# Decoding in the attention stage ordered for later transfers, a hand-over filled with input products, and output chains that go on as activations come

## The chip, the core and the metric

The kernel runs on one core of one Trainium2 chip. Five engines work side by side, each through a queue of its own: PE (TensorE, matmuls; its weight loads are PEld), DVE (VectorE), ACT (ScalarE), POOL (GpSimd) and SP (SyncE, which here only issues transfers). The metric is the device time of one execution in microseconds.

## What is computed

```python
def rmsnorm(x, g): return x / sqrt(mean(x * x, -1) + 1e-06) * g
q_n, k_n = rmsnorm(q, g_q), rmsnorm(k, g_k)            # (4, 12, 448, 64)
attn = softmax(q_n @ k_n.T / 8) @ v
x = attn.transpose(0, 2, 1, 3).reshape(1792, 768)
x = relu(x @ w_in) ** 2 @ w_out                        # layer 1: 768 -> 2048 -> 768
out = silu(x @ w_gate) * (x @ w_val) @ w_out2          # layer 2: 768 -> 1536 -> 768
```

Everything is float32. The products keep float32 accuracy: each operand is split into a rounded high part and a low rest, and each product is three matmuls (`mm3`: high by high, high by low, low by high).

## The kernel before

**Stages.** In the attention stage (0 to about 416 us) 24 pairs of heads are worked through: scores `sc`, a softmax whose exponentials go into `ring`, transposes `pt` that are copied into `turned_p`, the values product `o`, and `ox`, the normed result, which is stored and split into `x`. PE has time to spare there, and it is filled with layer 1's first six blocks of 128 inner columns for batches 0 to 2 (`fillers`, `ffn1a`: `h_a` and `ya`). Batch 3's blocks 0 to 2 end that filling (`lead`: `h_lead` twice, then `lead`). After this hand-over `products` finishes batch 3: for block `f` an input product `h`, a squared ReLU (`squares`: ReLU on ACT, L405; square on ACT, L406; ReLU times ReLU on DVE, L407, which frees the bank of `h`; the low rest on DVE, L411), and output products `y` into six banks (`first_out`). Then come 14 passes over what is left of layer 1 and all of layer 2, each over two batches at once with Strassen's seven products (`unit`: `p1` to `p7`, from sums of weights `s`, `a` and sums of tokens `t`, `b`). A pass ends with its output products (`outputs`): twelve chains of `y`, one for each of six column blocks `j` and two batches `h`. A chain adds up the contributions of all units of the pass, in the order of `deep`; the activation of a unit, row and batch is an `s_...` tile whose low part DVE writes last (L1691, layer 2: L1138).

**Word loads and decoding.** The weights arrive as 64-bit words. `word_chunk` loads 128 x 384 of them (`raw_...`, 384 KB, one of two buffers) and decodes them in place in four steps (L1163 or L1165, L1169, L1172, L1179); the last writes a part tile, of which `DEC_TEMPS` may be in use. `combine` adds part tiles (L1143) to the sums that the seven products need, and `keep` stores each part in DRAM, from where the passes read it back. `decode_ahead` does this for the passes' weights from the attention stage on, behind everything else.

**What sets the order.** The code is made of threads that ask for instructions with a cost each; a planner (`simulate`, `dispatch`) with a clock of its own hands them to the engines, lowest rank first, and the order in which it does so is the order of each engine's queue on the chip. An engine takes its queue strictly in this order. A transfer counts in the planner as `max(dma_free, clock + 1100) + bytes / 300 + 900 + later` ns: the fourth element of what `dma` yields is `later`, used once the attention stage has begun to lend PE to the fillers (`lent`). A thread that yields a condition goes on when it holds on the planner's clock. `ranked` is set at the hand-over.

**Names.** `led`, `DEC_LATER` and `AHEAD` do not exist yet. In `outputs` (L1711) the first four or six chains are begun up to the last element of `deep`, those of batch 0 first, then each chain is ended in turn. Eight banks of PSUM serve `p` and `y`; `h_free` lists the free ones.

Of the kernel before, what the change touches and what calls it, by code (L numbers as in the profile page):

```python
# [54 lines left out]
KEEP = {"q": 2, "x": 3, "p": 3, "y": 1, "u": 0}  # L55
DEC_AHEAD = 2
DEC_FROM = 0
DEC_TEMPS = 3
POOL_DMA = 900
POOL_LATER = 2500  # L60
BEHIND = 2
# [22 lines left out]
WC = 384  # L84
# [4 lines left out]
def attention_two_ffn_kernel(  # L89
# [77 lines left out]
    def spawn(gen, rank, is_local=False):  # L167
        t = Thread(gen, rank, is_local)
        local[is_local] += 1
        resume(t, None)  # L170
        return t
# [32 lines left out]
    port, port_last, ranked = [0.0], [], []  # L204
# [61 lines left out]
    def dma(issue, nbytes, later=0):  # L266
        while not ranked and nbytes >= DMA_BULK and dma_free[0] > clock[0] + 1100 + DMA_QUEUE:
            yield dma_free[0] - clock[0] - 1100 - DMA_QUEUE
        yield {"S": 475}, issue, nbytes, later if lent else 0
# [34 lines left out]
    wt, placed, seen = {}, {}, set()  # L304
# [84 lines left out]
    def h_tile(name):  # L389
        yield lambda: h_free  # L390
        where = h_free.pop(0)
        return tile_at(where, [128, S], F32, name), where
# [629 lines left out]
    def lead():  # L1022

        x = x1[B - 1]
        hs = []
        for f in range(2):
            hs.append((yield from h_tile(f"h_lead{f}")))
        parts = [(0, range(KD - 1)), (1, range(KD - 1)), (0, [KD - 1]), (1, [KD - 1]), (2, range(KD))]
        for n, (f, part) in enumerate(parts):
            if n == LEAD_HOLD:  # L1030
                leading.append(0)
            if f == 2:
                yield lambda: acc_last[0] == NH - 1 and t_banks
                where = t_banks.pop(0)
                hs.append((tile_at(where, [128, S], F32, "lead2"), where))
            for kk in part:
                yield lambda: kk in x
                yield from mm3(
                    hs[f][0], *wt["in", f], bass.ts(kk, 128), x[kk][:, 0, :], x[kk][:, 1, :], kk == 0, kk == KD - 1
                )  # L1040
            if part[-1] == KD - 1:
                spawn(squares(*hs[f], f"1_0_{f}"), 9000, FILL if f == 2 else False)
        yield lambda: "1_0_1" in ready
        leading.clear()

# [31 lines left out]
            h_free.append(next(w for w in t_banks if w[0] is ps_f))  # L1077
            t_banks.remove(h_free[-1])

    filled, lent = [], []  # L1080

    def all_stats():
        for b in range(B):
# [73 lines left out]
    def word_chunk(src, c, raw_at, name, parts):  # L1157
        src = src.bitcast(I32).rearrange("p (n two) -> p n two", two=2)
        raw = raw_at[0].tile([128, WC, 2], I32, tag=raw_at[1], name=f"raw_{name}")
        yield from dma(lambda e: e.dma_start(out=raw, in_=src[:, bass.ts(c, WC), :]), 8 * WC * 128)  # L1160
        high, low = raw[:, :, 1], raw[:, :, 0]
        yield {"A": 455, "W": 269}, lambda e: (
            e.activation(out=high.bitcast(F32), in_=high.bitcast(F32), func=ACTF.Copy, scale=2.0 ** -112)  # L1163
            if e is nc.scalar
            else e.tensor_scalar(  # L1165
                out=high.bitcast(F32), in0=high.bitcast(F32), scalar1=2.0 ** -112, scalar2=None, op0=ALU.mult
            )
        )
        yield {"W": 269}, lambda e: e.tensor_scalar(  # L1169
            out=low, in0=low.bitcast(U32), scalar1=2.0 ** -29, scalar2=7.0, op0=ALU.mult, op1=ALU.min  # L1170
        )
        yield {"W": 469}, lambda e: e.scalar_tensor_tensor(  # L1172
            out=low, in0=high, scalar=SIGN_BIT, in1=low, op0=ALU.bitwise_and, op1=ALU.bitwise_or
        )
        yield lambda: ahead_of[0] < DEC_TEMPS
        ahead_of[0] += 1
        at = yield from temp()
        t = tile_at(at, [128, WC], F32, name)
        yield {"W": 469}, lambda e: e.scalar_tensor_tensor(  # L1179
            out=t.bitcast(I32), in0=high, scalar=3, in1=low, op0=ALU.logical_shift_left, op1=ALU.bitwise_or  # L1180
        )
        raws.append(raw_at)
        parts[name] = t, at
# [18 lines left out]
        back(at)  # L1202

    def keep(key, name, t):
        yield from dma(lambda e: e.dma_start(out=pre_d[key][name], in_=t), 4 * WC * 128)
        kept.add((name, key))

    def keep_out(key, name, parts):
# [264 lines left out]
    def products():  # L1473
        k = POST
        xs = x1[LAST]
        behind, ys = [], {}
        for f in range(G1):
            name = f"1_0_{f}"
            if f < 3:
                release(("in", f))  # L1480
            else:
                ps, where = yield from h_tile(f"h_{name}")
                yield from in_product(ps, wt["in", f], xs)
                spawn(squares(ps, where, name), k - 2)
                release(("in", f))
            while len(behind) >= BEHIND:
                yield from behind.pop(0)
            behind.append(first_out(name, f, ys, k))
            k += 1
        for j in range(6):  # L1490
            s_free.append((xp, f"x{j}"))
        for gen in behind:
            yield from gen
        io_free.extend(ea_free)
        yield from all_passes()
        finished.append(0)
# [214 lines left out]
    def outputs(n, sums, drop_w, k):  # L1711
        layer, p, us = passes[n]
        deep = depth(layer, us)
        ahead = 4 if len(deep) > 2 else 6
        ys = {}
        y_order = order_of(n)
        last_use = {j // 3: m for m, (j, h) in enumerate(y_order)}

        def chain(j, h, part):
            ps = ys[j, h][0]  # L1720
            for u, r in part:
                name = f"o{2 * r + j // 3}"
                yield lambda: ((layer, u), name) in operand and (n, u, r, h) in ready
                w, s = operand[(layer, u), name][0], ready[n, u, r, h][0]
                yield from mm3(
                    ps, w[:, 0], w[:, 1], bass.ts(j % 3, 128), s[:, 0], s[:, 1],
                    (u, r) == deep[0], (u, r) == deep[-1],
                )

        for j, h in sorted(y_order[:ahead], key=lambda jh: jh[1]):  # L1730
            ys[j, h] = yield from bank_tile(f"y_{n}_{j}_{h}")
            yield from chain(j, h, deep[:-1])
        for m, (j, h) in enumerate(y_order):
            if m >= ahead:
                ys[j, h] = yield from bank_tile(f"y_{n}_{j}_{h}")
            yield from chain(j, h, deep[-1:] if m < ahead else deep)
            spawn(summed_out(n, j, h, ys[j, h], sums), k)
            if m == last_use[j // 3] and drop_w:
                for u, r in deep:
                    w_free.append(operand.pop(((layer, u), f"o{2 * r + j // 3}"))[1])  # L1740
        for u, r in deep:
            for h in range(2):
                s_free.append(ready.pop((n, u, r, h))[1])
# [118 lines left out]
```

## Time and profile before

| | |
|---|---|
| median of 3 runs | 1242.45 us (1241.45 to 1244.17) |
| profiled execution | 1242.65 us, span 1240.7 us |
| PE busy | 1199.1 us, 97% of the span, 6336 matmuls |
| DVE, ACT, POOL busy | 919.5, 705.0, 289.9 us |
| DMA | 271.69 MB, mean 219 GB/s |
| chain that ended last | PE 69%, DVE 10%, DMA 9%, ACT 7% |

A busy share is an average over stages. The page models the ends of matmuls: one of 448 columns is shown 0.37 us long while the next starts 0.20 us after it, so short pauses of PE do not all show. For an engine's wait the page names the instruction or transfer that came last before it.

### The profile page before, as it was taken

How to read it: one execution, taken by the hardware profiler on the slowest of the kernel's cores; microseconds unless marked ns; L12 is line 12 of the kernel's file. 1: busy time of each engine (PE TensorE's matmuls, PEld its weight loads, DVE VectorE, ACT ScalarE, POOL GpSimd, SP SyncE). 2: the span in 40 equal slices, each digit the busy share in tenths (PEclk: the TensorE clock that was granted, in tenths of full speed). 3: DMA queues.
4: the chain of work that ended last, by engine and by line, in shares of the span. 5: the costliest groups of instructions: out<-in, count | busy, mean ns of one | idle time of the engine just before them, and what ended most of it. 6: DMA issues, size and time to landing. Idle time of an engine off the chain costs nothing.

```text
span 1240.7 us, 20299 instructions
## 1 busy us (share of the span) xinstructions
PE 1199.1 (97%) x6336; PEld 1017.5 (82%) x6336; DVE 919.5 (74%) x1877; ACT 705.0 (57%) x1550; POOL 289.9 (23%) x411
## 2 busy tenths in 40 slices
PE   8989999999999899999999999999999999999998
PEld 6656667676767799999889989998999899989998
DVE  7998987786777697493659798786767577857744
ACT  6999877676767465454654353644453446344310
POOL 4454454433321002313430000110031305030000
PEclk9999999999999999999999999999999999999999
DMA  7576667667747879959897898967695889797714
GB/s 222 167 210 177 189 198 225 183 193 228 220 151 210 258 255 312 212 161 258 193 232 266 271 323 265 307 216 231 207 271 148 225 226 242 196 236 222 266 46 141
DMA packets 169694, 271.69 MB, mean 219 GB/s; under 512 B 25633, under 2 KB 149170, under 8 KB 169586
## 3 DMA queue, kind: packets, MB, share of 16 engines
q1 hardware_dynamic: 155762, 248.37, 63.4%
q0 software_dynamic: 13824, 22.03, 10.9%
q8 instruction: 50, 0.82, 0.3%
q14 instruction: 58, 0.48, 0.1%
HBM read 177.57 MB, written 92.74 MB: 218 GB/s over the span
## 4 chain that ended last, share of the span: by engine, by line
PE 69%; DVE 10%; DMA 9%; ACT 7%; issue 3%; SPq 1%; POOL 0%; DVEq 0%; ACTq 0%; POOLq 0%
PE p L370 32%; PE y L370 26%; ACT ring L808 3%; DMA raw_a<-in_w_in_dram 2%; PE ya L370 2%; PE o L937 2%; PE h_a L370 2%; PE sc L766 2%; DMA raw_o<-in_w_out_dram 2%; DVE sc L794 2%; ACT turned_p L262 1%; PE pt L897 1%; DMA a_d<-a 1%; PE h L370 1%; DMA nat<-in_k_n_dram 1%
## 5 line engine op out<-in xcount | busy, mean ns | idle before, releaser
L370 PE MATMUL y<-s,o_split 128*128 128x448 f32 x1584 | 326.2, 366 | 6.0 <-DVE s L1691 3.2
L370 PEld LDWEIGHTS y<-s,o_split 128*128 128x128 f32 x1584 | 296.8, 188 | 33.2 <-DVE s L1138 4.7
L1599 DVE TENSOR_TENSOR u<-p,u 128x448 f32<-128x448 f32 x204 | 124.2, 618 | 118.5 <-PE p L370 113.7
L370 PE MATMUL p<-t,s_split 128*128 128x448 f32 x918 | 205.4, 368 | 0.0
L370 PEld LDWEIGHTS p<-t,s_split 128*128 128x128 f32 x918 | 172.5, 188 | 16.2
L370 PE MATMUL p<-b,a_split 128*128 128x448 f32 x612 | 137.0, 368 | 0.0
L808 ACT ACTIVATE ring<-sc,m,rms 128x448 f32<-128x448 f32 x168 | 124.1, 743 | 8.8 <-DVE m L795 5.1
L370 PEld LDWEIGHTS p<-b,a_split 128*128 128x128 f32 x612 | 115.0, 188 | 10.5
L1759 ACT COPY yw<-y 128x448 f32<-128x448 f32 x120 | 63.3, 535 | 77.2 <-PE y L370 68.7
L794 DVE TENSOR_REDUCE sc<-sc 128x2 f32<-128x896 f32 (+1 forms) x96 | 93.7, 976 | 6.1 <-PE sc L766 5.2
L262 ACT COPY turned_p<-pt 128x384 f32<-128x384 f32 (+2 forms) x168 | 89.0, 544 | 13.5 <-PE pt L897 13.0
L897 PE MATMUL pt<-ident,ring 128*128 128x128 f32 x432 | 71.3, 276 | 9.3 <-DVE ox L959 4.9
L937 PE MATMUL o<-turned_p,v 128*64 128x448 f32 x384 | 79.8, 546 | 0.6 <-DVE turned_p L264 0.5
L370 PE MATMUL h_a<-x,hi_in 128*128 128x448 f32 x216 | 70.5, 389 | 0.0
L370 PE MATMUL ya<-sa,hi_out 128*128 128x448 f32 x216 | 69.5, 385 | 0.0
L897 PEld LDWEIGHTS pt<-ident,ring 128*128 128x128 f32 x432 | 52.0, 141 | 20.8 <-DVE ox L959 6.8
L370 PE MATMUL p<-t,a_split 128*128 128x448 f32 x306 | 68.8, 369 | 0.0
L370 PE MATMUL p<-b,s_split 128*128 128x448 f32 x306 | 68.3, 367 | 0.0
L1774 POOL DMA_DIRECT2D y2d<-yw x48 | 41.8, 919 | 92.3 <-ACT yw L1759 86.7
L370 PEld LDWEIGHTS p<-t,a_split 128*128 128x128 f32 x306 | 57.5, 188 | 5.7
L370 PEld LDWEIGHTS p<-b,s_split 128*128 128x128 f32 x306 | 57.5, 188 | 5.6
L1138 DVE TENSOR_TENSOR t<-t 128x448 fp32r<-128x448 f32 x87 | 50.6, 618 | 14.8 <-ACT t L262 14.6
(181 smaller groups left out, 2148.7 us busy)
## 6 DMA issues: line engine op xcount, KB each, us to landing
t<-t_d SPq DMA_DIRECT2D x96, 224.0 KB
raw_o<-in_w_out_dram SPq DMA_DIRECT2D x44, 384.0 KB
s_d<-a SPq DMA_DIRECT2D x68, 192.0 KB
s_split<-s_d SPq DMA_DIRECT2D x68, 192.0 KB
b<-x1d SPq DMA_DIRECT2D x51, 224.0 KB
kq<-in_kq_p_dram SPq DMA_DIRECT2D x23, 480.0 KB
y1d<-yw POOLq DMA_DIRECT2D x48, 224.0 KB, 7.7
y2d<-yw POOLq DMA_DIRECT2D x48, 224.0 KB, 7.2
```

Source lines behind the costliest of these rows:

```text
L262: e.copy(out, src)
L370: return {"P": 203}, lambda e: e.matmul(ps, lhsT=w, rhs=x, start=first, stop=last), 0
L766: e.matmul(parts[t][:, :S], lhsT=q[a][d, bass.ts(i % 4, 128)], rhs=k[c][d], start=(p == 0), stop=(p == len(passes) - 1),)
L794: e.tensor_reduce(out=top, in_=sc, axis=AX.X, op=ALU.max, negate=True)
L808: yield {"A": 704}, lambda e: e.activation(out=slot(i), in_=parts[t][:, :S], func=ACTF.Exp, bias=m[:, t:t + 1], scale=rq[:, i:i + 1], accu ...
L897: e.transpose(ps[:, bass.ts(j + (i > 3), 128)], p[:, bass.ts(j, 128)], ident)
L937: e.matmul(o[64 * h:64 * h + 64], lhsT=v[:, 4 * h + j], rhs=turned_p[:, 4 * h + j if j < 3 else 3], start=(j == 0), stop=(j == 3),)
L1138: yield {"W": 469 if c == WC else 535, "G": 956 if c == WC else 1106}, lambda e: e.tensor_tensor(out=t[:, 1], in0=plain, in1=as_f32(t[:, 0 ...
L1599: return {"V": 535}, lambda e: e.tensor_tensor(out=out, in0=ps, in1=b, op=ALU.add)
L1759: yield {"A": 424}, lambda e: e.copy(y, ps)
L1774: yield {"G": POOL_DMA}, lambda e: e.dma_start(out=dst, in_=y, accum_op=ALU.add), 2 * 128 * S * 4, POOL_LATER, True
```

## The change

Three things. **1.** `word_chunk` and `keep` pass `later = DEC_LATER = 1500` ns for their transfers until the hand-over, so that the planner takes them to land 1.5 us later; and four part tiles may be in use instead of three. **2.** `lead` adds the input product of block 3 of batch 3 behind the third lead chain and leaves its bank in `led`; `products` takes it from there when it comes to `f == 3`. **3.** `outputs` no longer begins a set number of chains: up to six chains are open; whenever an open chain's next activation and weights are there on the planner's clock, the oldest such chain goes on; else the next chain is opened if a bank is free.

```diff
-DEC_TEMPS = 3
+DEC_TEMPS = 4
+DEC_LATER = 1500
+AHEAD = 6
...  lead()
                 spawn(squares(*hs[f], f"1_0_{f}"), 9000, FILL if f == 2 else False)
+        ps, where = yield from h_tile("h_1_0_3")
+        yield from in_product(ps, wt["in", 3], x)
+        led.append((ps, where))
         yield lambda: "1_0_1" in ready
...  word_chunk()
-        yield from dma(lambda e: e.dma_start(out=raw, in_=src[:, bass.ts(c, WC), :]), 8 * WC * 128)
+        yield from dma(lambda e: e.dma_start(out=raw, in_=src[:, bass.ts(c, WC), :]), 8 * WC * 128, 0 if ranked else DEC_LATER)
...  keep()
-        yield from dma(lambda e: e.dma_start(out=pre_d[key][name], in_=t), 4 * WC * 128)
+        yield from dma(lambda e: e.dma_start(out=pre_d[key][name], in_=t), 4 * WC * 128, 0 if ranked else DEC_LATER)
...  products()
-                ps, where = yield from h_tile(f"h_{name}")
-                yield from in_product(ps, wt["in", f], xs)
+                if led:
+                    ps, where = led.pop()
+                else:
+                    ps, where = yield from h_tile(f"h_{name}")
+                    yield from in_product(ps, wt["in", f], xs)
...  outputs(): the two loops over y_order and chain() are replaced
+        todo, open_, left = list(order_of(n)), {}, {}
...
+        def can(j, h):
+            u, r = deep[open_[j, h][1]]
+            return ((layer, u), f"o{2 * r + j // 3}") in operand and (n, u, r, h) in ready
+
+        while todo or open_:
+            at = next((jh for jh in open_ if can(*jh)), None)
+            if at is None and todo and h_free and len(open_) < AHEAD:
+                at = todo.pop(0)
+                bank = yield from bank_tile(f"y_{n}_{at[0]}_{at[1]}")
+                open_[at] = [bank, 0]
+                continue
+            if at is None:
+                yield lambda: todo and h_free and len(open_) < AHEAD or any(can(*jh) for jh in open_)
+                continue
+            (j, h), ((ps, _), m) = at, open_[at]
+            u, r = deep[m]
+            w, s = operand[(layer, u), f"o{2 * r + j // 3}"][0], ready[n, u, r, h][0]
+            yield from mm3(ps, w[:, 0], w[:, 1], bass.ts(j % 3, 128), s[:, 0], s[:, 1], m == 0, m + 1 == len(deep))
+            open_[at][1] += 1
+            if m + 1 == len(deep):
+                spawn(summed_out(n, j, h, open_.pop(at)[0], sums), k)
```

PE has the same 6057 instructions in both. The orders are the same up to the eleventh pair of heads (about 182 us); from there on all engines' orders differ in places. Three places follow.

PE at the hand-over, before: `lead` is the third lead chain, whose last matmul takes block `x_23`; `y` are output products from activation `s_0_0` (block 0).

```order
L370 MATMUL lead_5783<-x_23_5663,hi_in_1118 128x448 x2
L370 MATMUL lead_5783<-x_23_5663,lo_in_1119 128x448
L370 MATMUL y_5855<-s_0_0_5779,hi_out_1836 128x448 x2
L370 MATMUL y_5855<-s_0_0_5779,lo_out_1837 128x448
L370 MATMUL y_5871<-s_0_0_5779,hi_out_1836 128x448 x2
```

PE at the hand-over, after the change; `h_0_3` is the input product of block 3.

```order
L372 MATMUL lead_5767<-x_23_5655,lo_in_1119 128x448
L372 MATMUL h_0_3_5808<-x_18_4717,hi_in_1364 128x448 x2
L372 MATMUL h_0_3_5808<-x_18_4717,lo_in_1365 128x448
...
L372 MATMUL h_0_3_5808<-x_23_5655,hi_in_1364 128x448 x2
L372 MATMUL h_0_3_5808<-x_23_5655,lo_in_1365 128x448
L372 MATMUL y_5856<-s_0_0_5762,hi_out_1836 128x448 x2
L372 MATMUL y_5856<-s_0_0_5762,lo_out_1837 128x448
```

The 18 matmuls of `h_0_3`, which stood behind the first six chains of `y`, now stand ahead of them.

DVE in the attention stage, ahead of the normed result `ox` of the twentieth pair, before: `raw_...` and `a_...` rows are decoding (L1169, L1172, L1179), `sa` a low rest of a filler.

```order
L411 TENSOR_TENSOR sa_1_4849<-r_a_1_4854,sa_1_4849 128x448
L1169 TENSOR_SCALAR raw_a_1_3_4722<-raw_a_1_3_4722 128x384
L1169 TENSOR_SCALAR raw_a_1_3_4785<-raw_a_1_3_4785 128x384
L1172 SCALAR_TENSOR_TENSOR raw_a_1_3_4722<-raw_a_1_3_4722 128x384
L1172 SCALAR_TENSOR_TENSOR raw_a_1_3_4785<-raw_a_1_3_4785 128x384
L1179 SCALAR_TENSOR_TENSOR a_1_3_4887<-raw_a_1_3_4722 128x384
L1179 SCALAR_TENSOR_TENSOR a_1_3_4889<-raw_a_1_3_4785 128x384
L959 TENSOR_TENSOR ox_4899<-o_4865,zb_4799 128x448
```

DVE at the same place after the change (lines are 2 to 5 higher: L1174, L1177, L1184 are the same decoding steps; `r_a` belongs to a filler).

```order
L1177 SCALAR_TENSOR_TENSOR raw_o_1_2_4699<-raw_o_1_2_4699 128x384
L409 SCALAR_TENSOR_TENSOR r_a_1_4842<-h_a_1_4741,r_a_1_4842 128x448
L1184 SCALAR_TENSOR_TENSOR o_1_2_4866<-raw_o_1_2_4699 128x384
L413 TENSOR_TENSOR sa_1_4838<-r_a_1_4842,sa_1_4838 128x448
L834 COPY ring<-ring 128x64
L1174 TENSOR_SCALAR raw_a_1_3_4755<-raw_a_1_3_4755 128x384
L1177 SCALAR_TENSOR_TENSOR raw_a_1_3_4755<-raw_a_1_3_4755 128x384
L1184 SCALAR_TENSOR_TENSOR a_1_3_4887<-raw_a_1_3_4755 128x384
L961 TENSOR_TENSOR ox_4897<-o_4864,zb_4804 128x448
```

Six rows of decoding from two chunks stood ahead of `ox`; now three rows from one chunk stand there, and the second chunk comes behind it.

PE at the start of the first pass's output products, before: `y_j_h` is the chain of column block `j` and batch `h`, `s_u_r_h` the activation of unit `u`, row `r` and batch `h`.

```order
L370 MATMUL y_0_0_6513<-s_0_0_0_6298,o_1_0_split 128x448 x3
L370 MATMUL y_0_0_6513<-s_0_1_0_6391,o_1_0_split 128x448 x3
L370 MATMUL y_0_0_6513<-s_1_0_0_6456,o_1_1_split 128x448 x3
L370 MATMUL y_1_0_6537<-s_0_0_0_6298,o_1_0_split 128x448 x3
L370 MATMUL y_1_0_6537<-s_0_1_0_6391,o_1_0_split 128x448 x3
L370 MATMUL y_1_0_6537<-s_1_0_0_6456,o_1_1_split 128x448 x3
L370 MATMUL y_0_1_6554<-s_0_0_1_6335,o_1_0_split 128x448 x3
L370 MATMUL y_0_1_6554<-s_0_1_1_6372,o_1_0_split 128x448 x3
L370 MATMUL y_0_1_6554<-s_1_0_1_6496,o_1_1_split 128x448 x3
```

PE at the same place after the change.

```order
L372 MATMUL y_0_1_6497<-s_0_0_1_6326,o_1_0_split 128x448 x3
L372 MATMUL y_0_1_6497<-s_0_1_1_6353,o_1_0_split 128x448 x3
L372 MATMUL y_0_0_6510<-s_0_0_0_6284,o_1_0_split 128x448 x3
L372 MATMUL y_0_0_6510<-s_0_1_0_6369,o_1_0_split 128x448 x3
L372 MATMUL y_0_0_6510<-s_1_0_0_6432,o_1_1_split 128x448 x3
L372 MATMUL y_0_1_6497<-s_1_0_1_6483,o_1_1_split 128x448 x3
L372 MATMUL y_1_1_6537<-s_0_0_1_6326,o_1_0_split 128x448 x3
L372 MATMUL y_1_1_6537<-s_0_1_1_6353,o_1_0_split 128x448 x3
L372 MATMUL y_1_1_6537<-s_1_0_1_6483,o_1_1_split 128x448 x3
```

`s_1_0_1` was first used behind 24 matmuls and is now first used behind 15; batch 1's chain is begun first.

## Rows read from the trace of the kernel before

**Rows 1.** Table by stretch: start:end, length, then busy us of each engine

```profile
core 0: us, PE busy (x) PEld busy (x) DVE busy (x) ACT busy (x) POOL busy (x), PEclk, DMA share, GB/s
...
182.20:416.40 234.20, 221.86 (x1300) 163.57 (x1299) 173.01 (x383) 162.23 (x392) 71.81 (x106) 0.99 0.68 205
416.40:431.90 15.50, 11.11 (x56) 9.96 (x54) 12.17 (x24) 8.19 (x17) 0.47 (x1) 1.00 0.85 269
431.90:492.30 60.40, 60.40 (x288) 55.50 (x289) 51.26 (x94) 34.87 (x73) 5.33 (x5) 0.97 0.83 275
492.30:1237.50 745.20, 738.80 (x3601) 675.50 (x3599) 518.17 (x982) 343.17 (x685) 124.06 (x132) 1.00 0.79 225
```

**Rows 2.** Table by stretch, short stretches; the third last number is the granted clock

```profile
200.00:220.00 20.00, 18.24 (x106) 13.86 (x106) 14.49 (x33) 14.40 (x37) 8.77 (x15) 1.00 0.73 225
...
347.00:350.60 3.60, 3.25 (x10) 3.00 (x11) 2.85 (x6) 3.27 (x9) 3.47 (x3) 0.53 0.67 176
...
432.60:436.00 3.40, 3.40 (x11) 2.99 (x11) 2.56 (x6) 0.95 (x2) 0.00 (x0) 0.51 1.02 329
```

**Rows 3.** Waits of PE, 182 to 420 us: us in total, times, longest

```profile
PE pt L897 <- DVE ox L959: 4.6, 3, 2.7
```

**Rows 4.** Waits of ACT, 182 to 420 us

```profile
ACT raw_o L1163 <- DMA raw_o<-in_w_out_dram: 22.4, 11, 6.4
...
ACT raw_a L1163 <- DMA raw_a<-in_w_in_dram: 12.0, 7, 3.9
```

**Rows 5.** Timeline of all engines, 338 to 348 us: start, us, instruction, idle before

```profile
338.58 0.98 SPq L1160 DMA_DIRECT2D raw_a<-in_w_in_dram  x2
...
343.46 0.58 ACT L1163 ACTIVATE raw_a<-raw_a 128x384 f32<-128x384 f32 x1 [3.90 <-DMA raw_a<-in_w_in_dram]
...
344.52 0.57 ACT L1163 ACTIVATE raw_a<-raw_a 128x384 f32<-128x384 f32 x1 [0.48 <-DMA raw_a<-in_w_in_dram]
...
346.68 0.61 DVE L959 TENSOR_TENSOR ox<-o,zb 128x448 f32<-128x448 f32 x1
...
347.35 0.47 PE L897 MATMUL pt<-ident,ring 128*128 128x128 f32 x1 [2.67 <-DVE ox L959]
```

**Rows 6.** Timeline of PE, 176 to 430 us, two rows behind a wait

```profile
184.71 0.66 PE L892 MATMUL pt<-ident,ring 128*128 128x128 f32 x4 [0.99 <-ACT rkr L635]
201.77 0.47 PE L766 MATMUL sc<-kst,qst 128*128 128x448 f32 x1 [1.73 <-ACT ring L808]
```

**Rows 7.** Timeline of all engines at the hand-over, 423 to 438 us

```profile
424.17 0.54 ACT L405 ACTIVATE r<-h_lead 128x448 f32<-128x448 f32 x1
...
427.13 0.37 PE L370 MATMUL lead<-x,lo_in 128*128 128x448 f32 x1
...
431.22 0.61 DVE L407 SCALAR_TENSOR_TENSOR r<-lead,r 128x448 f32<-128x448 f32 x1
...
431.89 0.68 PE L370 MATMUL y<-s,hi_out 128*128 128x448 f32 x2 [4.39 <-DVE r L407]
...
437.19 0.57 PE L370 MATMUL h<-x,hi_in 128*128 128x448 f32 x2
```

**Rows 8.** Timeline of PE at starts of output stages

```profile
492.30 7.86 PE L370 MATMUL y<-s,o_split 128*128 128x448 f32 x38
...
592.99 12.82 PE L370 MATMUL y<-s,o_split 128*128 128x448 f32 x62 [1.25 <-DVE s L1691]
...
1092.50 5.83 PE L370 MATMUL y<-s,o_split 128*128 128x448 f32 x28
1098.78 1.50 PE L370 MATMUL y<-s,o_split 128*128 128x448 f32 x6 [0.45 <-DVE s L1138]
...
1215.04 22.05 PE L370 MATMUL y<-s,o_split 128*128 128x448 f32 x108
```

**Rows 9.** Timeline of DVE in the first and the twelfth output stage

```profile
495.84 0.61 DVE L1691 TENSOR_TENSOR s<-c,s 128x448 fp32r<-128x448 f32 x1
...
1098.10 0.62 DVE L1138 TENSOR_TENSOR s<-u,s 128x448 fp32r<-128x448 f32 x1
```

More of the change, by code (lines that the diff above doesn't have):

```diff
@@ L1078, in warm @@
             t_banks.remove(h_free[-1])
-    filled, lent = [], []
+    filled, lent, led = [], [], []
     def all_stats():
@@ L1713, in outputs @@
         deep = depth(layer, us)
[L1714 to L1740, printed above, removed]
+        todo, open_, left = list(order_of(n)), {}, {}
@@ new lines, in outputs @@
+        for j, h in todo:
+            left[j // 3] = left.get(j // 3, 0) + 1
+        def can(j, h):
[18 more added lines that the diff above has]
+                spawn(summed_out(n, j, h, open_.pop(at)[0], sums), k)
+                left[j // 3] -= 1
+                if not left[j // 3] and drop_w:
+                    for u, r in deep:
+                        w_free.append(operand.pop(((layer, u), f"o{2 * r + j // 3}"))[1])
```

## Prediction

> **What bounds the kernel.** I read the table by stage first: TensorE (PE) is busy 221.9 of 234.2 us in the part of the attention stage that the change can reach (182.2 to 416.4 us), 11.1 of 15.5 us around the hand-over, and 738.8 of 745.2 us from the first output chains of the passes to its last matmul [rows 1]. The reader should see that PE is the bound everywhere and that its number of matmuls does not change, so all that can be won is time in which PE stands still or runs slowly. That is 12.3, 4.4 and 6.4 us in these three stretches. Next the granted clock: it is full except in two stretches of 3.4 us at half speed, the lower level of 1.2 GHz, one after 2.67 us without work and one after 4.39 us [rows 2, 5, 7]. Then who ends PE's waits in the attention stage: most of all DVE's ox, 4.6 us in three places [rows 3]. DVE is not slow there; ACT, ahead of it, waits 34.4 us in 18 places for the word loads raw_o and raw_a [rows 4]. The timeline of one place joins the two: a raw_a load is issued at 338.58 and lands at 343.46, ACT has stood 3.90 us before its decoding, DVE goes through two chunks of decoding, ox comes at 346.68 and PE goes on at 347.35 after 2.67 us [rows 5].
>
> The sum is made against the profiled execution, 1242.65 us (span 1240.7 and 1.95 us around it). The median of the three runs is 0.2 us lower, which I leave out.
>
> **Decoding ordered later.** The planner writes the engines' orders by its own clock, in which a load of 384 KB lands 1.1 + 1.31 + 0.9 = 3.3 us after issue. On the chip the load above took 4.88 us, and its twin, issued right behind it, landed at 344.52 [rows 5]. Adding 1.5 us to the planner's landing puts it at 4.8, so decoding moves behind other work that ACT and DVE have ready. SP keeps its transfers; the stores of parts move with the decoding that makes them, and one raw load falls behind the first loads of the passes, where nothing waits for it before layer 2. Six PE waits between 182 and 348 us end behind a decoding that waited for its load, the first 0.99 us at 184.71, the last the 2.67 us at 347.35, together 9.02 us [rows 5, 6]. For each of them the wait of ACT or DVE shrinks by up to 1.5 us, and six rows of decoding ahead of one ox become three (the order of DVE above). If every wait of PE shrank as its cause does, 7.5 us of the 9.02 would go. The clock: 1.73 us without work at 201.77 left it full, 2.67 us did not [rows 2, 6], so with the last wait under 1.7 us the slow stretch goes too. Slow running costs half of 3.4 us, measured better at the hand-over below: 1.65. Upper bound: 9.02 + 1.65 = 10.7 us won. Lower bound: the moved decoding meets another ox and makes new waits as fast as it removes old ones; one such wait of the size in rows 5, with its clock, costs 2.67 + 1.65 = 4.3 us. Between ends so far apart I take half of the nine, 4.5, and the slow stretch, 1.65: 6.2 us, because the new order has three places with four or more decoding rows in a row on DVE where the old one has ten, but ACT and DVE are left with the same amount of work.
>
> A fourth part tile lets a chunk finish its last step, and free its raw buffer, without waiting for the oldest part to be stored. The trace has no row of a chunk that waits for a tile. Its gain lies inside the 10.7 us and its price is the same 4.3 us per place if two chunks meet ahead of an ox; I give it nothing of its own. The stores of parts get the same 1.5 us; only rows of DVE wait for them and none of PE's six waits ends there, so I put them at nothing; uncovered, they would cost what a new wait costs, 4.3 us.
>
> Here the Trainium skill speaks against the change: SBUF — State Buffer, section The DMA setup-cost knee, puts a transfer at about 2 us and its bytes over 436 GB/s. For 384 KB that is an estimate of 2.9 us, under the planner's old 3.3, so nothing would be waited for and the later order would win nothing. By that rule the sum is that of the first rival below. The trace disagrees with 4.88 us, where the queue's other transfers run beside it.
>
> **Hand-over.** PE ends the third lead chain at 427.50, and starts the first y at 431.89, 4.39 us later, when DVE's r of the lead tile (431.22) has ended [rows 7]. The change puts the 18 matmuls of input block 3 between them. A matmul costs (22.05 - 0.37) / 107 = 0.203 us in a long run [rows 8], so 3.65 us: PE works until 431.15. They were needed later anyway and leave there. Their bank is that of the first lead chain, free after DVE's r of it. ACT has the ReLU of that chain at 424.17 [rows 7]; in the new DVE order no decoding stands ahead of r, so it can come at about 424.7, before 427.5. From there r of the third chain is eight DVE rows away. At 0.61 us a row, what r takes itself [rows 7], that is 4.9 us: it ends by 430.2, before 431.15. So the remaining 0.74 us go too. And as PE has no pause, the 18 y matmuls no longer take 437.19 - 431.89 = 5.30 but 3.65 us [rows 7]: 1.65 us more. Sum 6.04 us. If DVE's r comes late by the whole old delay, all of it stays: bounds 0 and 6.04, and I take 6.04 because each step has 0.9 us or more to spare. What is late next would be the operands of the first pass, for which PE does not wait at all between 431.9 and 492.3 [rows 1].
>
> **Output chains.** Seven waits of PE end with an activation s, from 1.25 us at 592.99 to 0.45 at 1098.78, 5.7 us together [rows 8]. The obvious estimate is that chains which go on as activations come remove them. But the new order also asks for the last activations sooner: in the first stage s_1_0_1 is used after 15 matmuls instead of 24. I took each of the fourteen stages: the end of every s on DVE, less the stage's start, less 0.203 us for each matmul ahead of its second use of it. First stage: s written 495.84 + 0.61 = 496.45, start 492.30, 4.15 us; the old order has 25 matmuls ahead, 5.08 us, and does not wait; the new one 16, 3.25 us, and waits 0.9 [rows 8, 9]. Last stage with a wait: s ends at 1098.10 + 0.62 = 1098.72, 6.22 us after 1092.50; 28 matmuls ahead in both orders, 0.53 late in both [rows 8, 9]. Summed, the old order is late by 7.3 us in six stages and the new one by 7.0 in seven: 0.3 us won. (The waits the profile shows are fewer because it models a matmul's end at 0.37 us.) Bounds: all 7.3 go if DVE's rows come sooner, or each of the fourteen stages waits half a microsecond more where DVE's order has changed, 7 us lost. I take 0.3.
>
> Sum: 1242.65 - 6.2 - 6.04 - 0.3 = 1230.1, so 1230.
>
> **Rivals.** 1. The later order wins nothing: loads land early enough, or other waits take the place of the six. Then 1242.65 - 6.04 - 0.3 = 1236.3. For it: ACT and DVE keep all their rows, and DVE is busy 173 of 234 us in that stretch [rows 1]. Against it: the 4.88 us [rows 5].
> 2. The hand-over wait stays because the bank or the ReLU comes late: a store of y waits ahead of the ReLU's tile. Then 1230.1 + 6.0 = 1236.1. Against it: 0.9 us or more to spare at each step [rows 7].
> 3. The output waits close as well, because more chains are open: 1230.1 - 7.0 = 1223.1. Against it: the count above, by which activations, not chains, are late.
> 4. Slower: with four part tiles, decoding bunches up on DVE ahead of ox. Each place like that of rows 5 costs 4.3 us. With nothing won in attention (1236.3), two more such places eat the hand-over's gain (1244.9), which is the point from which it decides; three make 1249.2. Against it: ten bunches of four or more rows become three.
>
> **Chances.** Forecast 0.52, with a range of its own from 1226 to 1235 (attention wins 10.7 to 1.5 us); rival 1 0.22; rival 2 0.08; rival 3 0.10; rival 4 0.08. The range of 8 in 10 runs from 1224 to 1240: the forecast with rivals 1 and 2, and the nearer part of rival 3. About 0.2%, 2.5 us, is what a measurement of this kernel can tell from no change; the three runs lie 2.7 us apart. Faster by more than that holds for the forecast, rivals 2 and 3 and nearly all of rival 1: 0.86. Within 0.2%: the rest of rival 1 and a mild rival 4, 0.07. Slower: 0.07.
>
> **What would show it.** Hand-over: h matmuls directly behind the third lead chain, no PE wait above 0.5 us before y, and the first 18 y matmuls in 3.7 us at full clock; a wait ending with r on the lead tile says rival 2. Attention: ACT's waits for raw loads well under 34 us, PE idle from 182 us to the hand-over near 7 instead of 12, no slow stretch; the same 12 us with other releasers says rival 1; more rows of decoding before ox, rival 4. Outputs: waits of PE for s still 5 to 6 us in all, with a new one in the first stage; none at all says rival 3. The forecast as a whole is wrong if the time is above 1240, or if PE's idle time moved to places that none of these steps names.

## The result and the profile after

The changed kernel takes 1224.89 us (median of 4 runs, 1223.32 to 1229.90) against 1241.95 us before: a ratio of 0.9868 (95% interval 0.9835 to 0.9900). The forecast was 1230, range 1224 to 1240. The profiled execution took 1229.90 us (span 1227.9), 12.75 less than the one of before, so the account below is of 12.75 us and not of the 17 between the medians. It is the slowest of the four runs; the other three took 1223.32 to 1225.75 us.

Table by stretch of the kernel after, cut at the same events as [rows 1] (first lead matmul, first y, first output chain, last matmul); columns as there:

```profile
core 0: us, PE busy (x) PEld busy (x) DVE busy (x) ACT busy (x) POOL busy (x), PEclk, DMA share, GB/s
182.20:412.95 230.75, 221.81 (x1301) 163.88 (x1298) 171.69 (x382) 160.18 (x389) 72.06 (x106) 0.99 0.67 206
412.95:427.70 14.75, 14.75 (x74) 13.67 (x73) 11.13 (x21) 8.62 (x17) 0.00 (x0) 1.00 0.77 255
427.70:482.66 54.96, 54.96 (x272) 50.58 (x271) 50.14 (x98) 33.04 (x70) 2.04 (x2) 1.00 0.92 301
482.66:1224.30 741.64, 738.07 (x3601) 675.52 (x3599) 520.21 (x984) 343.56 (x687) 124.41 (x134) 1.00 0.79 227
```

Against [rows 1], attention is 3.4 us shorter, with 8.9 us without work on PE where there were 12.3. The hand-over has no idle time at all: lead, product and first pass together are 6.2 us shorter. From the first output chain to the end of the last matmul (1237.09 us before, 1224.24 after), 3.5 us stay idle instead of 6.0, and the stretch is 3.2 us shorter. (The last row of [rows 1] runs 0.4 us past the last matmul; the 6.4 us read from it are 0.4 too many.) So 3.4 + 6.2 + 3.2 = 12.8.

**Hand-over.** Timeline of the kernel after, 423 to 428 us, which answers to [rows 7] (start, us, instruction, idle before):

```profile
423.70 0.36 PE L372 MATMUL lead<-x,lo_in 128*128 128x448 f32 x1
423.89 0.57 PE L372 MATMUL h<-x,hi_in 128*128 128x448 f32 x2
...
425.30 0.62 DVE L409 SCALAR_TENSOR_TENSOR r<-lead,r 128x448 f32<-128x448 f32 x1
...
427.34 0.36 PE L372 MATMUL h<-x,lo_in 128*128 128x448 f32 x1
427.55 0.56 PE L372 MATMUL y<-s,hi_out 128*128 128x448 f32 x2
```

The product h stands directly behind the third lead chain, and r of the lead tile has ended at 425.92, 1.6 us before PE asks for it. The first y matmuls run at full clock (427.70 to 431.40 us: 1.00).

**Attention.** Waits of PE, 182 to 420 us (us in total, times, longest), answering to [rows 3]:

```profile
PE pt L897 <- DVE ox L961: 2.5, 2, 2.2
PE sc L768 <- ACT ring L810: 2.1, 1, 2.1
PE pt L899 <- DVE ox L961: 1.2, 2, 0.8
```

Waits of ACT, 182 to 416 us, answering to [rows 4]:

```profile
ACT raw_a L1168 <- DMA raw_a<-in_w_in_dram: 10.4, 5, 4.4
ACT raw_o L1168 <- DMA raw_o<-in_w_out_dram: 9.8, 7, 3.0
```

and the longest of DVE there:

```profile
DVE kq L706 <- DMA rkb<-rkd: 10.0, 5, 3.4
```

ACT waits 20.2 us for word loads instead of 34.4, as the later planned landing should have it. The longest wait of PE is still 2.2 us, though, and still ends with ox. What is ahead of ox has changed. Timeline of DVE and PE, 288 to 295 us:

```profile
288.75 0.56 DVE L1177 SCALAR_TENSOR_TENSOR raw_a<-raw_a 128x384 int32<-128x384 int32 x1
292.75 0.69 DVE L706 SCALAR_TENSOR_TENSOR kq<-kq,gqk,rkb 128x448 f32<-128x448 f32 x1 [3.44 <-DMA rkb<-rkd]
...
294.20 0.62 DVE L961 TENSOR_TENSOR ox<-o,zb 128x448 f32<-128x448 f32 x1
...
294.87 0.33 PE L897 MATMUL pt<-ident,ring 128*128 128x128 f32 x1 [2.21 <-DVE ox L961]
```

Where a decoding row waited for a word load in [rows 5], now kq, the scaling of the next keys, waits 3.44 us for rkb (the factors from the keys' norms, loaded from DRAM), and ox stands behind it. In the kernel before DVE waited 2.4 us in this stretch for rkb, in the kernel after 10.0. Decoding has not gone from ahead of ox altogether: at 344.40 ACT goes on after 4.42 us of waiting for a raw load, three decoding rows and ox follow on DVE, and PE's wait of 0.80 us at 346.76 ends with that ox.

**Clock.** Table by stretch, two places of the kernel after (the third last number is the granted clock):

```profile
40.00:44.00 4.00, 3.34 (x17) 2.07 (x17) 3.37 (x9) 3.61 (x10) 3.23 (x11) 0.69 0.81 286
...
202.00:204.00 2.00, 1.92 (x6) 1.70 (x7) 1.74 (x6) 1.04 (x3) 0.54 (x2) 0.50 0.84 296
```

The slow stretches at 347 and 433 us [rows 2] are gone, but one has come at 41 us, where PE's waits from 38 to 42 us are those of before (1.13, 0.54, 0.32 us), and one at 202 us behind 2.07 us without work.

**Output chains.** Timeline of PE, the waits from 480 us on, answering to [rows 8]:

```profile
486.43 26.38 PE L372 MATMUL y<-s,o_split 128*128 128x448 f32 x128 [0.36 <-DVE s L1699]
585.10 12.83 PE L372 MATMUL y<-s,o_split 128*128 128x448 f32 x62 [1.83 <-DVE s L1699]
611.36 0.68 PE L372 MATMUL p<-t,a_split 128*128 128x448 f32 x2 [0.87 <-DVE t L1143]
841.75 17.08 PE L372 MATMUL y<-s,o_split 128*128 128x448 f32 x83 [0.17 <-DVE s L1143]
963.74 17.41 PE L372 MATMUL y<-s,o_split 128*128 128x448 f32 x83 [0.18 <-DVE s L1143]
```

Waits for s are 2.5 us instead of 5.7. The new one in the first stage is there (486.43), as forecast; the one in the third stage has grown from 1.25 to 1.83 us; those of the late stages have gone or shrunk, which was not forecast. A wait of 0.87 us for t, an input of the next pass, is new.

### The profile page after: what moved, and what is told of

Same layout as the page of the kernel before. It is cut to its first block, busy times and chain, and to the rows that moved or that the text cites. A ratio compares the mean times of both kernels' runs of the same rounds, so it can differ in the third digit from the quotient of the medians.

```text
span 1227.9 us, 20260 instructions
## 1 busy us (share of the span) xinstructions
PE 1197.9 (98%) x6336; PEld 1017.7 (83%) x6336; DVE 920.6 (75%) x1879; ACT 702.0 (57%) x1548; POOL 286.0 (23%) x409
## 3 DMA queue, kind: packets, MB, share of 16 engines
q0 software_dynamic: 13824, 22.03, 11.3%
## 5 line engine op out<-in xcount | busy, mean ns | idle before, releaser
L264 ACT COPY turned_p<-pt 128x512 f32<-128x512 f32 (+2 forms) x169 | 89.3, 540 | 21.4 <-PE pt L899 19.7
L939 PEld LDWEIGHTS o<-turned_p,v 128*64 128x64 f32 x384 | 27.3, 137 | 40.7 <-issue 33.5
```

Source lines behind the costliest of these rows:

```text
L264: e.copy(out, src)
L939: e.matmul(o[64 * h:64 * h + 64], lhsT=v[:, 4 * h + j], rhs=turned_p[:, 4 * h + j if j < 3 else 3], start=(j == 0), stop=(j == 3),)
```

## The experiments

To compare the traces I cut each at four events: the start of the twelfth pair's product with v, the first lead matmul, the first output chain, the end of the last matmul. In the trace of before these are 196.22, 416.39, 492.30 and 1237.09 us, so three stretches: A (attention from the twelfth pair) 220.2 us, B (hand-over and first pass) 75.9, C (output stages and passes) 744.8. "chains" are the new output chains, "b/t" the edit of the group "Curing the second place". "rows" counts the decoding rows of DVE (those that read a raw tile) from the start to the first lead matmul. Each A, B, C and count is of one profiled execution; the intervals are of all runs of a kernel against runs of before made beside them.

| kernel | ratio to before (95%) | A | B | C | rows |
|---|---|---|---|---|---|
| before | 1 | 220.2 | 75.9 | 744.8 | 150 |
| after | 0.9868 (0.9835-0.9900) | 216.8 | 69.7 | 741.6 | 150 |
| e1 later landing alone | 0.9900 (0.9878-0.9922) | 208.7 | 72.2 | 745.1 | 140 |
| e2 fourth tile alone | 1.0015 (0.9997-1.0033) | 223.8 | 76.9 | 744.6 | 151 |
| e3 product alone | 0.9966 (0.9951-0.9982) | 221.4 | 71.6 | 745.0 | 150 |
| e4 chains alone | 1.0014 (0.9992-1.0036) | 218.4 | 75.2 | 743.4 | 152 |
| e5 after, again | 0.9862 (0.9839-0.9886) | 211.2 | 69.7 | 741.9 | 150 |
| e6 after, three tiles | 0.9894 (0.9872-0.9916) | 207.2 | 69.7 | 751.9 | 140 |
| e7 later + product | 0.9866 (0.9844-0.9887) | 209.3 | 69.7 | 746.9 | 140 |
| e8 as e6, 2.5 us later | 0.9951 (0.9930-0.9971) | 208.7 | 69.7 | 757.7 | 138 |
| e9 as e6, b/t later | 0.9836 (0.9810-0.9862) | 206.6 | 69.7 | 740.4 | 140 |
| e10 after, b/t later | 0.9853 (0.9827-0.9878) | 210.9 | 69.7 | 739.5 | 150 |
| e11 after without chains | 0.9874 (0.9846-0.9902) | 211.8 | 69.7 | 743.7 | 151 |
| e12 as e7, b/t later | 0.9869 (0.9843-0.9895) | 206.7 | 69.7 | 745.6 | 140 |

### One part at a time

e1, the later landing:

```diff
+DEC_LATER = 1500
-... dma(lambda e: e.dma_start(out=raw, ...), 8 * WC * 128)
+... dma(lambda e: e.dma_start(out=raw, ...), 8 * WC * 128, 0 if ranked else DEC_LATER)
-... dma(lambda e: e.dma_start(out=pre_d[key][name], in_=t), 4 * WC * 128)
+... dma(lambda e: e.dma_start(out=pre_d[key][name], in_=t), 4 * WC * 128, 0 if ranked else DEC_LATER)
```

> The kernel before with the 1.5 us on the planned landing of decoding transfers alone; part tiles stay three, hand-over and output chains as before. By the forecast's step the whole of the decoding's gain is here: 6.2 us less than the kernel before beside it (ratio 0.9950), the hand-over wait of PE near 4.4 us and the seven output waits stay. Rival A, the later order wins nothing: within 1 us of before. Rival B, it needs the fourth part tile to move anything: about half, 3 us (0.9975).

Measured: 12 us less than before (ratio 0.9900), twice the forecast's size for the whole decoding, and above its upper bound of 10.7. A is 11.5 us shorter. ACT's waits for word loads, 182 to 420 us, add up to 18.2 us instead of the 34.4 of [rows 4]:

```profile
ACT raw_o L1164 <- DMA raw_o<-in_w_out_dram: 9.7, 6, 2.1
ACT raw_a L1164 <- DMA raw_a<-in_w_in_dram: 8.5, 6, 2.6
```

From 205 us to the hand-over PE waits three times, 0.64, 0.36 and 0.33 us. Its idle time in A falls from 11.3 to 3.1 us: of the six waits that the bound had counted only the one behind the ring stays, and the others shrank with them. The other 3.3 us of the 11.5 lie in PE's busy time and are not broken down. Something besides the landing time has changed, too: 140 decoding rows stand ahead of the hand-over instead of 150. Ten rows, some 6 us of DVE, have moved behind it, and C is no longer for that (745.1 us, 744.8 before). No run separates how much of the 11.5 us comes from the better order and how much from the smaller load on DVE, nor the loads from the stores in `keep`, which got the same 1.5 us. And the hand-over's wait, which the forecast left whole, fell from 4.39 to 2.26 us. PE of this kernel:

```profile
199.76 0.47 PE L767 MATMUL sc<-kst,qst 128*128 128x448 f32 x1 [1.78 <-ACT ring L809]
288.44 0.66 PE L893 MATMUL pt<-ident,ring 128*128 128x128 f32 x4 [0.64 <-ACT turned_p L263]
...
416.98 0.68 PE L371 MATMUL y<-s,hi_out 128*128 128x448 f32 x2 [2.26 <-DVE r L408]
```

e2, the fourth tile (`DEC_TEMPS = 3` to `4`):

> The kernel before with four part tiles alone, no later landing. The forecast gave this part nothing of its own: within 1 us of before (0.999 to 1.001). Rival B, the tile is half of the decoding's gain: 3 us less (0.9975). Rival 4 of the prediction, decoding bunches up ahead of ox: 4 us more (1.0035).

Measured: the ratio is 1.0015, not apart from 1, and A is 3.6 us longer. The tile wins nothing; what it costs, this run doesn't settle.

e3, the product in the hand-over (the `led` lines of the diff alone):

> The kernel before with the input product of block 3 in the hand-over alone. By the forecast's step: 6.0 us less than before (0.9951): no PE wait above 0.5 us between the third lead chain and the first y, and the 18 y matmuls in 3.7 us instead of 5.3. Rival, the gain is only the idle time and the slow clock comes in another place: 4.4 us less (0.9965). Rival 2, the wait stays: within 1 us.

Measured: 4.2 us less, where the rival had 4.4, but only the number agrees: at the hand-over the idle time did not go whole. The slow stretch at 433 us has gone (one has come at 618 us), but two waits of 0.56 and 0.84 us for DVE's r stay around the product, since without the later landing DVE comes late to r. So B is only 4.3 us shorter, not 6.2. In every kernel with both parts it is 69.7. The two parts share the old wait: later landing alone 3.7, product alone 4.3, both 6.2.

e4, the chains (`outputs()` of the changed kernel alone):

> The kernel before with the output chains going on as activations come, alone. By the forecast's count of late activations: 0.3 us less than before (0.9998), 5 to 6 us of waits for s on PE stay, one of about 0.9 us new in the first output stage. Rival C, read from the trace of the changed kernel, in which the time from the first output chain to the last matmul is 3.2 us shorter: 3 us less (0.9974), and the waits go in the last nine stages, the first five lose about 1.9 us as in that trace. Rival D, what the trace gained there came from other stages having moved and not from the chains: within 0.5 us and the old waits unchanged.

Measured: 1.0014, not apart from 1. C is 1.4 us shorter, and the waits for s that stay are 1.25, 0.23 and 0.70 us, so they do go; two waits for t of 0.77 and 1.39 us are new. The time alone would say rival D, the trace says half of rival C.

### Does the fourth tile hurt?

e5 is the changed kernel; e6 has `DEC_TEMPS = 3` in it; e7 is e1 and e3 together; e8 is e6 with `DEC_LATER = 2500`.

> The changed kernel once more, beside the three that follow, for a second profile of it. Theory N (the 3.4 us that its first profile won in attention is one execution's luck, that of the later order alone won 13.4): attention 9 us or more shorter than in the trace of before, time 0.987 of before. Theory H (the fourth part tile takes back what the later order wins): attention again only 3 to 5 us shorter, time 0.987 to 0.990.

> The changed kernel with three part tiles instead of four, all else as changed. Theory N: within 2 us of the changed kernel beside it (ratio to before 0.986 to 0.988). Theory H: 4 us or more faster than it (ratio to before 0.983 or less), attention 12 us or more shorter than before.

> The kernel before with the later landing and the input product in the hand-over; three part tiles, output chains as before. The later order alone left 2.3 us of PE wait at the hand-over, so the product can win at most that and a slow stretch of 1.65 us: 2.3 to 3.9 us less than the later order alone, ratio to before 0.987 to 0.988. If the two gains simply add (6 us by the forecast, 4.2 us by the run with the product alone): 0.985 to 0.987. Against the three-tile kernel with all the rest it says what the output chains are worth: theory D, nothing within 1 us; theory C, 3 us.

> The changed kernel with three part tiles and a planned landing 2.5 us later instead of 1.5. In the trace of the changed kernel raw loads land 3.7 to 6.4 us after issue where ACT stood waiting for them, the planner with 1.5 us takes 4.8: if later is better as long as a load can still be late, it wins another 1 to 2 us against 1.5 (attention has some 1 to 3 us of wait behind decoding left); if the order is past its best, decoding bunches up later and it loses 2 to 4 us.

Measured: both theories fall as a whole. In attention the kernels with the tile are slower: A is 216.8 and 211.2 us in the two profiles with four tiles, 207.2, 209.3 and 208.7 with three. The count of rows differs with it: with the later landing and three tiles 138 to 140 decoding rows stand ahead of the hand-over, with four 150, as many as before. So the fourth tile brings back the ten rows that the later landing had moved out. Yet e6 is no faster than the changed kernel but rather 4 us slower (1229.4 us, 1225.6 of the changed kernel beside it; the intervals overlap a little), because its C is 10 us longer: the sixth output stage took 39.35 us instead of 29.35. Timelines of PE, DVE and ACT of e6 there:

```profile
710.58 0.57 ACT L264 CAST t<-t 128x448 fp32r<-128x448 f32 x1 [1.82 <-DMA t<-t_d]
...
714.94 0.63 DVE L1143 TENSOR_TENSOR t<-t 128x448 fp32r<-128x448 f32 x1 [1.41 <-ACT t L264]
...
721.40 0.62 DVE L1763 TENSOR_TENSOR yp<-y,yp 128x448 f32<-128x448 f32 x1
...
722.07 12.78 PE L372 MATMUL y<-s,o_split 128*128 128x448 f32 x48 [5.95 <-DVE yp L1763]
```

yp is the sum that frees a finished chain's bank. It stands behind the splitting of b and t, the next passes' inputs, and some of these wait for their loads: the fault that the change cures in attention, in a place where it is not cured. Of the 15.1 us from the stage's last s (706.27) to yp, DVE stands still for 3.2; the rest is the rows themselves, which take 0.54 us each without a wait. In the changed kernel the same way takes 5.9 us, without a wait. The slow clock that follows (0.67 and 0.50 from 720 to 728 us) makes it 10. Between the stage's last s and its first yp, DVE's order has

```
changed:       b b b t t b b t t t                              yp
e6:            o b b t b t b t b t b b b t t a t t t t          yp
e9 (below):    b b t t b b b                                    yp
```

Where many rows stand there, PE waits for yp, though not in proportion: with 10 rows (the changed kernel) and 8 (e1) it has no such wait, with 20 (e6) 5.95 us, with 23 (e7) 4.10, with 26 (e8) 9.21. e7 is 4 us faster than e1 by the ratios, but their intervals overlap, and B accounts for 2.5 us. The comparison of e6 with e7, which was to price the chains, is spoilt by this wait in both. e8 shows that it is not later that is better: A is no shorter than with 1.5 us.

### Curing the second place

e9 and e10: the loads of b and t planned 1.5 us later as well, with three and four tiles. e11: the changed kernel with the old `outputs()`. e12: e7 with the edit of e9.

```diff
-    def split_in_place(t, src, c):
+    def split_in_place(t, src, c, later=0):
-        yield from dma(lambda e: e.dma_start(out=plain, in_=src), 4 * c * 128)
+        yield from dma(lambda e: e.dma_start(out=plain, in_=src), 4 * c * 128, later)
...
-            yield from split_in_place(t, src, S)
+            yield from split_in_place(t, src, S, 1500)
```

> The changed kernel with three part tiles, and the loads of a later pass's input quarters and sums (b and t) planned 1.5 us later as well. Theory O (the three-tile kernel loses 10 us in its sixth output stage, 39.35 instead of 29.35 us, because DVE's order has 20 rows of b and t, which come over late loads, ahead of the first sum yp that frees a bank; with this edit 8 rows stand ahead): that stage takes 30 us again, no wait of PE for yp, and the kernel is 7 to 10 us faster than the three-tile kernel before it, ratio to before 0.981 to 0.984. Rival P, the stage is bound by the transfers themselves, since PE comes to it 12 us sooner: the wait stays, or comes at another place of the same stage, ratio 0.987 to 0.991.

> The changed kernel (four part tiles) with the same later landing of b and t. Its sixth stage had no such wait (29.35 us, 10 rows ahead; now 8). Theory H2 (the fourth tile costs 4 to 9 us in attention, and the changed kernel is as fast as it is only because its order in the sixth stage came out well): attention 3 to 7 us shorter than before, ratio 0.985 to 0.988, and 4 us or more slower than the kernel with three tiles beside it. Theory N2 (the fourth tile costs nothing): within 2 us of it.

> The changed kernel with the output chains of before: later landing, four tiles and the product in the hand-over. In its sixth stage 9 rows stand ahead of the first yp. By the forecast's step it is 0.3 us slower than the changed kernel (0.987); theory C, which takes the 3 us of the two profiles as the chains' own: 3 us slower (0.989); theory E, the chains bring nothing and what the profiles gained there came from the order of DVE: within 1 us or faster (0.986 or less).

> Later landing of decoding, product in the hand-over, later landing of b and t; three tiles, output chains of before. By theory O the sixth stage, 36.88 us in the kernel without the last edit, takes 30 to 31 us: 6 us faster than that kernel, ratio 0.981 to 0.984. Against the first kernel of this group it says what the output chains are worth: theory C 3 us slower than it, theory E within 1 us.

Measured: e9 bears out theory O, except that a wait for yp is left. Its sixth stage takes 31.02 us instead of 39.35, and the wait is

```profile
718.63 7.57 PE L372 MATMUL y<-s,o_split 128*128 128x448 f32 x36 [1.41 <-DVE yp L1763]
```

instead of 5.95. It does not end with the first yp, which has the 7 rows ahead of it, but with the second, behind 14 more rows of t, b, a and s. DVE of e9 (the last line shows two sums, the first of which PE waits for):

```profile
708.90 0.62 DVE L1763 TENSOR_TENSOR yp<-y,yp 128x448 f32<-128x448 f32 x1 [1.36 <-DMA yp<-y1d]
...
717.96 1.15 DVE L1763 TENSOR_TENSOR yp<-y,yp 128x448 f32<-128x448 f32 x2
```

So the fault has become smaller and moved to the next sum, and the first sum now waits for a load of its own. The ratio falls from 0.9894 to 0.9836, 7 us, by an edit that only reorders, while the bytes are the same: the transfers as such did not set the 39 us, which speaks against rival P. Its table by stretch, attention first and the output stages last:

```profile
182.20:402.81 220.61, 217.83 (x1299) 163.34 (x1298) 168.36 (x375) 158.31 (x384) 70.36 (x105) 1.00 0.68 206
...
472.51:1212.90 740.39, 737.42 (x3601) 675.83 (x3599) 524.48 (x995) 342.63 (x688) 118.62 (x128) 1.00 0.80 229
```

In attention PE is without work for 2.8 us, where the kernel before had 12.3 and the changed kernel 8.9. At 1220.12 us e9 is the fastest kernel measured, though its interval overlaps that of the changed kernel.

e10 against e9: A is 4.2 us longer with four tiles, in the direction of theory H2; the times (1222.25 and 1220.12 us) agree in sign, but do not settle it, and theory H2's sizes do not hold (4 us or more slower than e9, attention 3 to 7 us shorter than before; A is 9.3 shorter). e11 against the changed kernel: C is 2 us longer without the chains, the times are not apart. e12 against e9: without the chains C is 5.2 us longer and the kernel 4 us slower, with overlapping intervals. But e12 missed its expected ratio: its sixth stage fell from 36.88 to 32.00 us, while a wait for t of 2.49 us came at 604.73, where e7 had none, and a slow stretch behind it. These two are some 4 of the 5.2 us, so this pair does not price the chains either.

## Why the prediction was right, and where it was not

- **The time.** 1230.1 was worked out against the profiled execution and 1229.9 came, with two errors of 3 us that cancelled: attention won 3.4 and not 6.2, the output stages 3.2 and not 0.3. That is luck, and also luck of which execution was profiled. The second profile (e5, 1227.0) has 9.0 us won in A, 6.2 in B and 2.9 in C, and comes to its twelfth pair 2.3 us later than before, with three slow stretches at 42 to 87 us, ahead of everything that the change moves. Between the medians the gain is 17 us where the three terms of the forecast add up to 12.5; the median, 1224.9, lies just inside the range and nearer to rival 3's 1223.1 than to 1230.
- **Decoding ordered later: right mechanism, parts wrong.** "I give it nothing of its own" is the step that failed, of the fourth tile. The later landing by itself wins 11.5 us of A (e1), above the bound of 10.7; with the fourth tile beside it A is 211 to 217 us in four profiles, 207 to 209 in the six without it. The times do not show this cost. The forecast also took ACT and DVE to be left with the same amount of work: that holds for the changed kernel (150 decoding rows ahead of the hand-over, as before), not with three tiles (140). The ten bunches of decoding that were to become three do not come out of the traces: DVE has six unbroken runs of four or more decoding rows from 182 us to the hand-over before, five in the changed kernel and three in e1. PE's idle time from 182 us to the hand-over, forecast near 7 us, is 8.9 and 6.0 us in the two profiles of the changed kernel.
- **What the tile costs, and through what.** Rival 4 was right about the sign of the tile. For the larger waits, though, what is late next is not decoding but kq behind rkb: DVE's waits for rkb up to 412 us are 10.0, 7.9, 7.5 and 6.2 us in the four profiles with both parts (after, e5, e10, e11), 3.7 to 4.4 in the five with three tiles and 1.5 us (e1, e6, e7, e9, e12). At about 255 us, in all four, kq waits 2.0 to 3.4 us, ox follows 1.55 us behind it, and PE's wait that ends with that ox is 0.34, 1.79, 1.08 and 0.96 us. That is a part of the tile's 2 to 10 us in A. No run moved kq alone or gave a four-tile kernel ten rows less, so the share of each stays open. By the forecast's own sign of being wrong, idle time in places that none of its steps names, this is such a place: the longest wait of PE in the changed kernel stands behind kq.
- **Rival 1, that the later order wins nothing.** e1 alone won 12 us, so it falls. In the trace after, a load that ACT stood waiting for was issued at 231.00 and decoded from 235.87, 4.87 us later (the line shows it and its twin). By the Trainium skill's page SBUF — State Buffer, section The DMA setup-cost knee, such a load would take about 2.9 us, an estimate from its fit; the trace does not agree.

```profile
231.00 0.98 SPq L1165 DMA_DIRECT2D raw_a<-in_w_in_dram  x2
...
235.87 0.57 ACT L1168 ACTIVATE raw_a<-raw_a 128x384 f32<-128x384 f32 x1 [2.37 <-DMA raw_a<-in_w_in_dram]
```

- **Hand-over: right.** 6.04 forecast, 6.2 measured in every kernel with both parts. The share of the product is smaller than credited: behind e1 it adds 72.2 - 69.7 = 2.5 us, and the later landing brings the other 3.7. Rival 2 did not come.
- **Output chains: mis-sized.** 0.3 forecast; C is 739.5 to 743.4 us in the five kernels with chains and no wait above 1.5 us for yp (mean 741.4), and 743.7 to 745.6 in the six with neither (mean 744.8): 3.4 us, or 2.9 without the slow stretches of 1.7 us that lie in C of e3, e5, e11 and e12. The count of matmuls ahead was right for the first stage (0.9 forecast; the stage is 0.8 longer than before; in e6 and e9, with the same chains, it is not longer). It failed because it set the new order of PE against the old times of DVE. In the twelfth stage, forecast late by 0.53 in both orders, the last s ends 5.53 us after the stage's start and not 6.22 [rows 8, 9], which the 28 matmuls ahead of it (5.68 us) cover. Between the row u<-u,u and that s, DVE has five rows before and three after. Before (the s is in [rows 9]):

```profile
1095.41 0.62 DVE L1674 TENSOR_TENSOR u<-u,u 128x448 f32<-128x448 f32 x1
```

After:

```profile
1081.87 0.62 DVE L1607 TENSOR_TENSOR u<-p,u 128x448 f32<-128x448 f32 x1
1082.40 1.22 DVE L1177 SCALAR_TENSOR_TENSOR raw_a<-raw_a 128x384 int32<-128x384 int32 x1
1083.54 0.61 DVE L1682 TENSOR_TENSOR u<-u,u 128x448 f32<-128x448 f32 x1
...
1085.55 0.61 DVE L1143 TENSOR_TENSOR s<-u,s 128x448 fp32r<-128x448 f32 x1
```

  So rival 3 was half true. How much of the 3.4 is the chains and how much DVE's order beside them stays open.
- **The slow clock.** "With the last wait under 1.7 us the slow stretch goes too" was a rule from two waits, and does not hold (last section).
- **What stays open.** The spread of one kernel, 1223.3 to 1229.9 us, is as wide as the smaller parts. Chains and fourth tile show in the stretches of the traces, one profile of each kernel, and the times alone do not tell them from nothing.

## What to carry to other kernels

Where a planner writes fixed orders, a transfer that it believes too fast is paid for by whoever stands behind the waiting row; look for the row that waits for a transfer ahead of the row that the bound engine needs, cure its landing time, and look for the next such row. Parts of such a change do not add: each moves the order everywhere, and here one place 300 us further on (20 rows ahead of a sum instead of 10) took back 10 us and hid what the rest had won. Compare kernels by the stretches between the same events before comparing their times, since a stretch shows a loss that another stretch's gain covers; and count the rows in each stretch, since a new order can also move work out of it.

## What the runs showed of the hardware

The granted clock does not follow the length of one wait (half is the lower level, 1.2 GHz). Behind the wait for the ring at about 200 us it stayed full after 1.73 us (before), 1.99 (e4) and 1.54 (e5), and fell to half after 1.62 (e7), 1.78 (e1), 2.07 (after) and 2.19 us (e2). In the trace after, the 2.21 us at 294.87 left it full. At 41 us, ahead of everything that the change moves, nearly the same waits of PE (1.13, then 0.52 to 0.55, then mostly 0.3 us) left it full in before, e1, e2, e6 and e11 and halved it in after, e3, e4, e5, e7, e8, e9, e10 and e12. A slow stretch of 3.4 us cost 1.65 us at the hand-over of before. Such stretches are a part of what separates two executions of one kernel here: over the 29 runs of before beside e1 to e4 the mean granted clock is 0.990 to 0.999, and the slower runs have the lower clock (correlation -0.72). They are not all of it: the four runs of the changed kernel, 6.6 us apart, have 0.997 or 0.998.
